# Nine chunks of 64 keys in quarters of the array, five score banks, probabilities turned in place and moved by pairs of units

## Chip, cores, metric

The kernel runs on one core of a Trainium2 chip. The metric is the device time of one execution in microseconds (us). The kernel before has a median of 1205.0 us in three runs (1204.82 to 1205.19).

## What is computed

Thresholded attention over 8 batches and 8 heads with 576 tokens and a head width of 64, followed by a mixer: a token MLP (576 to 256 to 576) and a channel MLP (512 to 1536 to 512), each with a residual. All data are fp32.

```python
scores = scale * np.matmul(q, k.transpose(0, 1, 3, 2))
thresh = np.max(scores, axis=-1, keepdims=True) - tau
scores = np.where(scores >= thresh, scores, -1000000000.0)
...
attn = attn / (np.sum(attn, axis=-1, keepdims=True) + 1e-09)
return np.matmul(attn, v).astype(np.float32)
...
xt = x.transpose(0, 2, 1)
h = np.maximum(xt @ w_tok1, 0.0) @ w_tok2
u = x + h.transpose(0, 2, 1)
h2 = np.maximum(u @ w_ch1, 0.0) @ w_ch2
return (u + h2).astype(np.float32)
```

## The kernel before

**Units, rounds, groups.** Heads are taken two at a time: a pair is two heads, whose 64 channels each lie on partitions 0 to 63 and 64 to 127. Two pairs of a batch have 9 units of 128 queries; the fifth (SHARED) holds the last 64 queries of one pair and the first 64 of the next. Two units are a round (72 in all), three units are a group (six to a batch, 48 in all).

**A round.** `scores_of_two` (L894) multiplies on PE: for each unit, three pieces of 192 keys, both heads, into two tiles of three banks, one for each head; six of the eight PSUM banks are the scores'. A product has 64 rows of the array (one head) and 128 columns; where a round has the shared unit, all its products are cut to 64 columns, that is into quarters of the array. fp32 products run in two passes, and the trace has two records for each. Then DVE takes the maxima, a round and head at a time (L927), POOL makes the bias (L933), ACT subtracts and masks out of PSUM (L943, `mask`) and takes the exponential in place with its sum (L953, `exps`); DVE inverts the sums, POOL scales (L285, `scale`). `e` then has 128 queries on the partitions and 2 x 576 keys.

**Turning e.** In batch 0 PE transposes `e` in blocks of 128 into a bank, and ACT or DVE copies it (L300, L305). In batches 1 to 7 DVE transposes 32x32 blocks from `e` into another tile `T` (L315, `turn_blocks`), and SP issues four transfers of 144 KB for each unit from `T` to `eT` (L327, `move`), after which the partitions hold keys.

**Values.** `values` (L350) makes the weighted sums of a group in one bank: output partitions 0 to 63 for one head, 64 to 127 for the other. A product contracts over 128 keys and fills 64 columns of the array, so that two run side by side. Since 576 keys are four and a half times 128, the fifth chunk of both heads shares one 128-row tile: it is multiplied by a copy of V in which the other head's rows are zero (`split_middle`, L333; its products stand at L365, the others at L370). The middle group of three covers two pairs and does this twice with 192 queries, the others once with 384. ACT or DVE copies the bank out (`values_out`, L372). V is loaded once for each pair, in batches 1 to 7 by four transfers in rows of 256 bytes (L128).

**Order.** Nothing is left to run time: a planner written into the kernel (`Scheduler`) keeps a clock for each engine, starts the earliest operation by the costs and dependencies written beside it, and emits the instructions in that order; the engines then run their queues in order. The mixer of the batch before (token MLP L477 to L515, channel MLP L1067 and L1143) fills PE between rounds and groups, through the two banks that the scores leave. While the planned clock is under 110 us, `keep_warm` (L719) fills planned gaps of PE with transposes (L732). After the last batch's attention the scores' banks go to the rest of the channel MLP (L1528), which the change does not touch.

## Time and profile before

| what | us |
|---|---|
| median of three runs | 1205.0 |
| the profiled execution | 1205.03 |
| its span on the core | 1203.2 |
| PE matmul busy | 1181.3 |
| DVE busy | 898.3 |
| ACT busy | 603.0 |
| POOL busy | 332.6 |

Some lines of the costliest groups (line, engine, operation, output and input by name and shape, count; then busy us, mean ns of one; then idle time before them and what ended it):

```profile
L943 ACT ACTIVATE e<-sc,bias 128x576 f32<-128x576 f32 x288 | 193.9, 743 | 148.9 <-POOL bias L933 147.8
L927 DVE TENSOR_REDUCE mx<-sc 128x2 f32<-128x1152 f32 x144 | 188.1, 1347 | 54.3 <-PE sc L910 54.3
L953 ACT ACTIVATE e<-e,ntau 128x576 f32<-128x576 f32 x288 | 220.4, 779 | 0.1
L315 DVE STREAM_TRANSPOSE T<-e 128x1152 f32<-128x1152 f32 x126 | 170.7, 1363 | 30.7 <-POOL e L285 23.3
```

And from the table of DMA issues (count, size of each, median us from issue to landing):

```profile
eT<-T SPq DMA_DIRECT2D x504, 144.0 KB, 3.0
```

PEld is the loading of weights into PE, which overlaps PE. Matmul records overlap too: two or four products that use different parts of the array run at once, so the mean of one record is not what it costs; the distance between starts is. In an engine's queue an instruction that waits holds up all behind it.

### The profile page before, as it was taken

The numbers are of one execution on the slowest core, as the hardware profiler recorded it, in microseconds if no ns is written. First come the engines' busy times: TensorE is split into PE (matmuls) and PEld (weight loads), VectorE is DVE, ScalarE is ACT, GpSimd is POOL, SyncE is SP. The second block draws the span as 40 slices with busy tenths as digits, with TensorE's granted clock in tenths as the row PEclk, the third lists the DMA queues.
The fourth block names the chain that finished last, engine by engine and source line by source line (L and its number), as shares of the span: only waits on it lengthen the run. The fifth ranks groups of instructions, "written<-read, shape, count | busy, mean of one in ns | idle before, by whom it ended". The sixth has DMA issues, their size and how long they took to land.

```text
span 1203.2 us, 22528 instructions
## 1 busy us (share of the span) xinstructions
PE 1181.3 (98%) x8177; PEld 966.2 (80%) x8177; DVE 898.3 (75%) x1547; ACT 603.0 (50%) x1363; POOL 332.6 (28%) x523
## 2 busy tenths in 40 slices
PE   8888999999999999999999999999999999999998
PEld 7656788777777777776877777787899999999988
DVE  6788996768678768767867855873778587776866
ACT  6988864664566565465555554550232413223230
POOL 3676553334233434433423422330100000000000
PEclk9999999999999999999999999999999999999999
DMA  7656987668778777777876875571310302122020
GB/s 150 131 134 149 246 198 163 153 137 184 171 153 177 184 159 165 191 159 160 204 155 154 185 182 113 148 181 45 92 36 10 86 12 71 36 51 56 16 56 35
DMA packets 327214, 153.03 MB, mean 127 GB/s; under 512 B 224000, under 2 KB 319296, under 8 KB 326976
## 3 DMA queue, kind: packets, MB, share of 16 engines
q1 hardware_dynamic: 324944, 150.86, 54.4%
q8 instruction: 65, 1.06, 0.4%
q10 hardware_dynamic: 2160, 0.74, 0.2%
q14 instruction: 45, 0.37, 0.1%
HBM read 48.50 MB, written 14.68 MB: 53 GB/s over the span
## 4 chain that ended last, share of the span: by engine, by line
PE 90%; DVE 3%; ACT 3%; DMA 2%; issue 1%; POOL 1%; SPq 1%; DVEq 0%; ACTq 0%; POOLq 0%
PE bank L1528 29%; PE bank L1143 14%; PE bank L1067 11%; PE sc L910 11%; PE bank L370 9%; PE bank L508 5%; PE bank L477 4%; PE bank L365 3%; PE bank L1158 2%; DVE mx L927 1%; ACT e L943 1%; DMA w2s<-in_moe_w_tok_dram 1%; ACT e L953 1%; PE bank L490 1%; DMA lk<-in_k_dram 1%
## 5 line engine op out<-in xcount | busy, mean ns | idle before, releaser
L285 POOL TENSOR_SCALAR e<-e,rr 128x576 f32<-128x576 f32 x288 | 217.0, 771 | 188.7 <-DVE rr L277 188.1
L943 ACT ACTIVATE e<-sc,bias 128x576 f32<-128x576 f32 x288 | 193.9, 743 | 148.9 <-POOL bias L933 147.8
L927 DVE TENSOR_REDUCE mx<-sc 128x2 f32<-128x1152 f32 x144 | 188.1, 1347 | 54.3 <-PE sc L910 54.3
L953 ACT ACTIVATE e<-e,ntau 128x576 f32<-128x576 f32 x288 | 220.4, 779 | 0.1
L315 DVE STREAM_TRANSPOSE T<-e 128x1152 f32<-128x1152 f32 x126 | 170.7, 1363 | 30.7 <-POOL e L285 23.3
L1143 PE MATMUL bank<-xT,wc 128*128 128x256 f32 x768 | 176.4, 383 | 0.3
L1143 PEld LDWEIGHTS bank<-xT,wc 128*128 128x128 f32 x768 | 143.3, 190 | 31.0 <-issue 7.0
L910 PE MATMUL sc<-kT,qT 64*128 64x192 f32 (+1 forms) x2112 | 162.4, 329 | 1.6 <-ACT e L943 1.0
L910 PEld LDWEIGHTS sc<-kT,qT 64*128 64x128 f32 (+1 forms) x2112 | 138.4, 167 | 27.7 <-issue 16.7
L370 PE MATMUL bank<-eT,lv 128*64 128x384 f32 (+1 forms) x1024 | 135.0, 406 | 0.0
L370 PEld LDWEIGHTS bank<-eT,lv 128*64 128x64 f32 x1024 | 73.5, 137 | 50.7 <-issue 45.3
L933 POOL TENSOR_SCALAR bias<-mx,toff 128x2 f32<-128x2 f32 x144 | 41.0, 286 | 194.6 <-DVE mx L927 189.6
L1067 PE MATMUL bank<-wc,g 128*128 128x256 f32 x336 | 77.7, 381 | 0.0
L1643 ACT COPY temps<-bank 128x256 f32<-128x256 f32 x90 | 33.5, 372 | 85.5 <-PE bank L1528 85.0
L508 PE MATMUL bank<-w,a 128*128 128x192 f32 (+1 forms) x256 | 72.6, 420 | 1.5 <-ACT eT L305 0.6
L1067 PEld LDWEIGHTS bank<-wc,g 128*128 128x128 f32 x336 | 62.9, 190 | 11.0 <-issue 1.6
L1148 ACT ACTIVATE g<-bank 128x256 f32<-128x256 f32 x58 | 22.2, 383 | 96.1 <-PE bank L1143 95.9
L1528 PE MATMUL bank<-t,wc 128*128 128x256 f32 x240 | 60.0, 379 | 0.0
L1528 PE MATMUL bank<-t,w1s 128*128 128x256 f32 x240 | 60.0, 379 | 0.0
L1528 PE MATMUL bank<-u,wc 128*128 128x256 f32 x240 | 59.8, 379 | 0.0
L508 PEld LDWEIGHTS bank<-w,a 128*128 128x128 f32 x256 | 43.1, 189 | 20.7 <-issue 5.0
L953 ACT ACTIVATION_READ_ACCUMULATOR e<-e,ntau 128x1 f32 x288 | 58.8, 204 | 0.0
(190 smaller groups left out, 1840.3 us busy)
## 6 DMA issues: line engine op xcount, KB each, us to landing
eT<-T SPq DMA_DIRECT2D x504, 144.0 KB, 3.0
w2s<-in_moe_w_ch_dram SPq DMA_DIRECT2D x24, 512.0 KB, 4.0
lk<-in_k_dram SPq DMA_DIRECT2D x122, 72.0 KB, 2.9
ut<-us SPq DMA_DIRECT2D x136, 64.0 KB, 2.1
lq<-in_q_dram SPq DMA_DIRECT2D x120, 72.0 KB, 3.1
lv<-in_v_dram SPq DMA_DIRECT2D x112, 72.0 KB, 2.6
out_dram<-us SPq DMA_DIRECT2D x30, 256.0 KB, 2.3
u<-spill SPq DMA_DIRECT2D x8, 512.0 KB, 4.5
```

The lines of the kernel that those rows point to most:

```text
L285: nc.gpsimd.tensor_scalar(out=eh, in0=eh, scalar1=rr[:, h : h + 1], scalar2=1.0, op0=ALU.mult, op1=ALU.mult)
L315: nc.vector.transpose(out=T.rearrange("p a (c x) -> p c a x", c=NK), in_=e.rearrange("p (c a x) -> p c a x", c=NK, a=4))
L370: nc.tensor.matmul(to[r], lhsT=lv[:, j, :], rhs=e[j], start=False, stop=(c == NI - 1), skip_group_check=True)
L477: nc.tensor.matmul(bank[:, at], lhsT=w1[:, t, P * m : P * m + P], rhs=x(t), start=(n == 0 and t == 0), stop=False, skip_group_check=True,)
L508: nc.tensor.matmul(bank[:, n * i : n * i + n], lhsT=hidden[b][:, m, P * c : P * c + P], rhs=w2[:, m, lo : lo + n], start=(m == 0), stop=(m ...
L910: nc.tensor.matmul(sc[h][rows, f, HT * k : HT * k + HT], lhsT=qT[r, cols], rhs=kT[r, HT * f : HT * f + HT], start=True, stop=True, skip_gr ...
L927: nc.vector.tensor_reduce(out=mx[:, h], in_=sc[h][:, :, 0 : 2 * HT].rearrange("p f (k x) -> p k f x", k=2), axis=AX.XY, op=ALU.max)
L943: nc.scalar.activation(out=eh, in_=part[h], func=AF.Prelu, bias=bias[:, h], scale=SCALE, alpha=STEEP)
L953: nc.scalar.activation(out=eh, in_=eh, func=AF.Exp, bias=ntau, accum_out=rs[:, h, 0:1])
L1067: nc.tensor.matmul(bank[:, 0:HD], lhsT=x[:, j, :], rhs=y[:, j, :], start=j == 0, stop=j == HJ - 1)
L1143: nc.tensor.matmul(bank[:, 0:n], lhsT=wc1[:, j, c, :], rhs=uT[:, c, GR * i : GR * i + n], start=(c == 0), stop=(c == NCC - 1))
L1528: nc.tensor.matmul(to, lhsT=l, rhs=r, start=start and x == 0, stop=x == len(pairs) - 1, skip_group_check=not start)
```

## The change

In batches 1 to 7 the keys are put in another order: K is transposed so that `e` has, for each of 4 x 9 blocks, 16 keys of one head beside 16 of the other. After the turn and the move a chunk has 64 keys of one head on partitions 0 to 63 and the same 64 of the other head on 64 to 127: nine chunks without a rest. `values_of_halves` multiplies each chunk in four products at a time: two heads (rows of the array) by two halves of 192 queries, into two banks. For the second half of a group the heads are crossed, which `side` and `crossed` see to, so that each quarter of the array is used once; V is loaded as it stands and crossed, each by two transfers in rows of 2304 bytes (`load_heads`), and `split_middle` remains for batch 0 alone. Two copies take the halves out.

All scores are made in quarters of the array, by cuts of 128, 384 and 64 keys (64, 384, 128 for the second unit), into one tile of five banks. The third bank holds keys of both heads; a POOL memset (`mark`) stands between the first unit's products there and the second's. The general banks become three. A mask of a round's second unit also waits for the second maximum.

`e` is turned in place and `T` goes; `e` is kept until the move has read it. Units of a batch come in another order, in which two of three rounds hold the first and third unit of a group: these share a tile and are moved together by four transfers. The planner's new operation takes two banks at once.

```diff
-    ps_s2 = attn.enter_context(tc.tile_pool(name="ps_s2", bufs=2, space=bass.MemoryType.PSUM, side="right", reuse_waits="tile"))
+    ps_s2 = attn.enter_context(tc.tile_pool(name="ps_s2", bufs=1, space=bass.MemoryType.PSUM, side="right", reuse_waits="tile"))
...
-    units = [(b, 2 * w, t) for b in range(B) for w in range(NP // 2) for t in range(9)]
+    first_row = [(2 * w, t) for w in range(NP // 2) for t in range(9)]
+    in_turn = (0, 2, 1, 4, 3, 5, 6, 8, 7)
+    paired = [(0, t) for t in in_turn] + [(2, t) for t in (1, 0, 2, 3, 5, 4, 7, 6, 8)]
+    units = [(b, *x) for b in range(B) for x in (paired if b else first_row)]
+    where = {x: u for u, x in enumerate(units)}
...
-                in_=(q, k)[which][b, 2 * p + h, 32 * lo : 32 * hi, 32 * c : 32 * c + 32].rearrange("(n t) d -> t n d", t=32),
+                in_=(q, k)[which][b, 2 * p + h, 32 * lo : 32 * hi, 32 * c : 32 * c + 32].rearrange(
+                    "(t n) d -> t n d" if which and b else "(n t) d -> t n d", t=32
+                ),
...
+    def place_v(name):
+        return att.tile([P, NK, D], F32, tag="lv", bufs=VL + 1, name=name)
...
-        lv = att.tile([P, NK, D], F32, tag="lv", bufs=VL, name=f"lv_{n}")
+        if n not in vals:
+            vals[n] = place_v(f"lv_{n}")
         rows = v[b].rearrange("h s d -> (h s) d")[2 * S * p : 2 * S * p + 2 * S, :]
-        if not b:
-            nc.sync.dma_start(out=lv, in_=rows.rearrange("(c p) d -> p c d", p=P))
-        else:
-            for a in range(4):
-                nc.sync.dma_start(out=lv[a:P:4], in_=rows.rearrange("(c a r) d -> a r c d", a=4, r=32)[a])
-        vals[n] = lv
-
+        nc.sync.dma_start(out=vals[n], in_=rows.rearrange("(c p) d -> p c d", p=P))
+
+    def load_heads(n, crossed):
+
+        b, p = pairs[n]
+        lv = quads[n, crossed] = place_v(f"lv_{n}_{crossed}")
+        for i in range(2):
+            rows = v[b, 2 * p + (1 - i if crossed else i)].rearrange("(a y c) d -> y a (c d)", y=16, a=4)
+            nc.sync.dma_start(out=lv[D * i : D * i + D].rearrange("p c d -> p (c d)"), in_=rows)
+
+    quads = {}
...
+            if which and in_blocks(pairs[n][0]):
+                nc.vector.transpose(
+                    out=heads[n][1].rearrange("p (a c z y) -> p y c a z", a=4, c=NK, z=8),
+                    in_=loaded[n][1].rearrange("p (y c) (a z) -> p y c a z", y=2, a=4),
+                )
+                continue
...
+    def side(u, h):
+        b, p0, t = units[u]
+        return 1 - h if in_blocks(b) and t % GU == 2 else h
+
+    def half(u, e, h):
+        if not in_blocks(units[u][0]):
+            return e[:, S * h : S * h + S]
+        at = 16 * side(u, h)
+        return e[:, :, :, at : at + 16]
...
+    def home_of(u):
+        it, k = divmod(u, 2)
+        if not in_pairs(it):
+            e = att.tile([P, 4, NK, 32], F32, tag="e1", bufs=EM, name=f"e_{u}")
+            return e if in_blocks(units[u][0]) else e.rearrange("p a c x -> p (a c x)")
+        if not k:
+            two[it] = att.tile([P, 4, 2, NK, 32], F32, tag="e2", bufs=EP, name=f"e_{u}")
+        if in_blocks(units[u][0]):
+            return two[it][:, :, k]
+        return two[it].rearrange("p a k c x -> p (a k c x)")[:, 2 * S * k : 2 * S * k + 2 * S]
+
+    EP, EM = 2, 3
...
+    def in_pairs(it):
+        b, p0, t = units[2 * it]
+        return t % GU != 1 if in_blocks(b) else it % 3 != 1
...
-        b, p0, t = units[u]
-        e = st.pop(u)
-        T = Ts[u] = att.tile([P, 4, NK * 32], F32, tag="T", bufs=3, name=f"T_{u}")
-        nc.vector.transpose(
-            out=T.rearrange("p a (c x) -> p c a x", c=NK), in_=e.rearrange("p (c a x) -> p c a x", c=NK, a=4)
-        )
-
-    def move(u):
-        b, p0, t = units[u]
+        e = st[u].rearrange("p a c x -> p a (c x)")
+        nc.vector.transpose(out=e, in_=e)
+
+    def move(us):
+        b, p0, t = units[us[0]]
-        T = Ts.pop(u)
+        if len(us) == 2:
+            e = two[us[0] // 2].rearrange("p a k c x -> p a (k c x)")
+            place = slice(0, GU, 2)
+        else:
+            e = st[us[0]].rearrange("p a c x -> p a (c x)")
+            place = t % GU
         for i in range(4):
-            nc.sync.dma_start(
-                out=turned_e[key][:, place, i, :], in_=T[32 * i : 32 * i + 32]
-            )
+            nc.sync.dma_start(out=turned_e[key][:, place, i, :], in_=e[32 * i : 32 * i + 32])
+        for u in us:
+            st.pop(u)
...
-            if n < NP:
-                nc.gpsimd.tensor_copy(out=vl[r, r], in_=lv[r, NI, :])
-            else:
-                nc.vector.tensor_tensor(
-                    out=vl[:, r].bitcast(I32), in0=lv[:, NI, :].bitcast(I32), in1=whose[:, r], op=ALU.bitwise_and
-                )
+            nc.gpsimd.tensor_copy(out=vl[r, r], in_=lv[r, NI, :])
...
+    HALVES = [((0, 0), (0, HT)), ((0, 2 * HT), (1, 0)), ((1, HT), (1, 2 * HT))]
+
+    def values_of_halves(b, p0, g, banks):
+        lv = [quads[b * NP + p0 + i, half] for half, (i, _) in enumerate(HALVES[g])]
+        M = HT // 32
+        for c in range(NK):
+            for half in range(2):
+                to = banks[half][:, 0:HT].rearrange("p (m x) -> p m x", x=32)
+                for i in range(2):
+                    r, o = [slice(D * x, D * x + D) for x in (i, 1 - i if half else i)]
+                    nc.tensor.matmul(
+                        to[o],
+                        lhsT=lv[half][r, c, :],
+                        rhs=eT[r, M * half : M * half + M, c, :],
+                        start=c == 0,
+                        stop=c == NK - 1,
+                        skip_group_check=True,
+                    )
+
+    def half_out(b, p0, g, half, bank, copy):
+        i, tok = HALVES[g][half]
+        copy(out=xTs[b][:, p0 + i, tok : tok + HT], in_=bank[:, 0:HT])
...
-    sched.banks.extend([Bank(ps_b, "m0"), Bank(ps_b, "m1")])
+    sched.banks.extend([Bank(ps_b, f"m{i}") for i in range(3)])
...
+    def make_heads(Q, m):
+        n = 2 * Q + m // 2
+        if Q < 2 or n >= len(pairs):
+            return
+        free = {0: 3 * Q - (1 if Q == 2 else 2), 1: 3 * Q - (2 if Q == 2 else 1), 2: 3 * Q - 1, 3: 3 * Q}[m]
+        heads_loaded[0] = put(
+            ("heads", Q, m),
+            sched.op("sp", 1.2, lambda: load_heads(n, 1 - m % 2), (key_op("V", free),), 0, after=(heads_loaded[0],), dmas=(2, 147, 0.70)),
+        )
...
+    AT = (0, 5 * MAIN - 2 * S)
+    CUTS = ((0, P, MAIN, S), (0, D, D + 3 * P, S))
+
+    mark = const.tile([P, 1], F32, name="mark")
+
     def scores_of_two(us):
-        sc = [ps_s2.tile([P, 3, MAIN], F32, tag="sc", name=f"sc{h}_{us[0]}") for h in range(2)]
-        split = any(units[u][2] == SHARED for u in us)
+
+        sc = ps_s2.tile([P, 5 * MAIN], F32, tag="sc", name=f"sc_{us[0]}")
+        firsts = []
         for k, u in enumerate(us):
             b, p0, t = units[u]
-                n, step = b * NP + p0 + (t > SHARED), D if split else P
-                parts = [(n, slice(o + i, o + i + step), slice(i, i + step)) for i in range(0, P, step)]
-            for f in range(3):
-                for n, cols, rows in parts:
+                parts = [(b * NP + p0 + (t > SHARED), slice(o + i, o + i + D), slice(i, i + D)) for i in (0, D)]
+            crossed = [in_blocks(b) and t % GU == 1 and i == 1 for i in range(2)]
+            for lo, hi in zip(CUTS[k], CUTS[k][1:]):
+                for c, ((n, cols, rows), cross) in enumerate(zip(parts, crossed)):
                     for h in range(2):
                         r = slice(D * h, D * h + D)
                         qT, kT = heads[n]
-                        nc.tensor.matmul(
-                            sc[h][rows, f, HT * k : HT * k + HT],
+                        slot = 1 - h if cross else h
+                        at = AT[slot] + S * k
+                        x = nc.tensor.matmul(
+                            sc[rows, at + lo : at + hi],
                             lhsT=qT[r, cols],
-                            rhs=kT[r, HT * f : HT * f + HT],
+                            rhs=kT[r, lo:hi],
                             start=True,
                             stop=True,
                             skip_group_check=True,
                         )
+                        if (at + lo) // MAIN == 2:
+                            if k:
+                                behind(x, marked)
+                            else:
+                                firsts.append(x)
+            if not k:
+                marked = nc.gpsimd.memset(mark, 0.0)
+                for x in firsts:
+                    behind(marked, x)
...
-            out=mx[:, h], in_=sc[h][:, :, 0 : 2 * HT].rearrange("p f (k x) -> p k f x", k=2), axis=AX.XY, op=ALU.max
+            out=mx[:, h], in_=sc[:, AT[h] : AT[h] + 2 * S].rearrange("p (k x) -> p k x", k=2), axis=AX.X, op=ALU.max
...
-            e = att.tile([P, 2 * S], F32, tag="e", bufs=4, name=f"e_{u}")
+            e = home_of(u)
-        eh = e[:, S * h : S * h + S].rearrange("p (f x) -> p f x", f=3)
-        nc.scalar.activation(out=eh, in_=part[h], func=AF.Prelu, bias=bias[:, h], scale=SCALE, alpha=STEEP)
+        scores = part[h]
+        if in_blocks(units[u][0]):
+            scores = scores.rearrange("p (a c y) -> p a c y", a=4, c=NK)
+        nc.scalar.activation(out=half(u, e, h), in_=scores, func=AF.Prelu, bias=bias[:, h], scale=SCALE, alpha=STEEP)
...
+        if in_blocks(b):
+            deps += [key_op("heads", G // 3, m) for m in (g, g + 1)]
+            if p0 == 0 and g == 0:
+                deps += xreads.get(b - 2, [])
+            x = put(("V", G), sched.op("pe", VALUES_IN_HALVES, lambda: None, deps, 0))
+            x.fn, x.bank, x.both, x.values = lambda banks: values_of_halves(b, p0, g, banks), True, True, True
+            for half in range(2):
+                y = sched.op(
+                    "act",
+                    0.33,
+                )
+                y.frees, y.half = x, half
+                put(("X", G) if half else ("X", G, 0), y)
+            next_heads(G)
+            return
...
-                    deps += [key_op("T", u - 4), key_op("pre", u - 1, 0)]
+                    deps += used_before(u) + [key_op("pre", u - 1, 0)]
                 else:
                     deps.append(key_op("pre", u, 0))
+                if u % 2:
+                    deps.append(key_op("mx", it, 1))
...
-            put(("T", u), sched.op("dve", 1.31, lambda u=u: turn_blocks(u), deps, 4))
-            put(
-                ("M", u),
-                sched.op(
+            put(("T", u), sched.op("dve", 1.31, lambda u=u: turn_blocks(u), deps + [key_op("T", u - 1)], 4))
+            space = [key_op("V", G - 2) if opens or in_pairs(it) else None]
+            if not in_pairs(it) or u % 2:
+                ws = (u - 1, u) if in_pairs(it) else (u,)
+                x = sched.op(
                     "sp",
                     2.4,
-                    lambda u=u: move(u),
-                    (key_op("T", u), key_op("V", G - 2) if t % GU == 0 else None),
+                    lambda ws=ws: move(ws),
+                    [key_op("T", w) for w in ws] + space,
                     0,
-                    after=(key_op("M", u - 1),),
-                    dmas=(4, 147, 0.69),
-                ),
-            )
-            if t % GU == GU - 1:
+                    after=(key_op("M", ws[0] - 1),),
+                    dmas=(4, 147 * len(ws), 0.69),
+                )
+                for w in ws:
+                    put(("M", w), x)
```

## The prediction

> **What bounds the kernel now.** I read the stages first (busy time of each engine in chosen windows), since a mean over the whole span mixes stages with different limits. The columns are the window, its length, busy time and count for PE, PEld, DVE, ACT and POOL, then the granted clock, the DMA share and GB/s.
>
> ```profile
> 0.00:150.00 150.00, 133.10 (x1049) 99.45 (x1051) 126.74 (x216) 125.84 (x264) 86.11 (x132) 1.00 0.71 162
> 203.00:789.00 586.00, 585.18 (x4089) 450.09 (x4089) 433.01 (x611) 334.76 (x725) 210.22 (x344) 1.00 0.74 165
> 852.00:1203.00 351.00, 347.06 (x2256) 322.50 (x2254) 266.61 (x626) 99.51 (x278) 0.00 (x0) 1.00 0.17 46
> ```
>
> From 203 to 789 us PE idles for 0.8 of 586 us; no other engine is above 74%. Only before 150 us does PE idle (17 us), with DVE and ACT both near 84%. After 852 us no attention runs, and the change leaves that part alone. The chain that ended last says the same:
>
> ```profile
> PE 90%; DVE 3%; ACT 3%; DMA 2%; issue 1%; POOL 1%; SPq 1%; DVEq 0%; ACTq 0%; POOLq 0%
> ```
>
> So between 150 and 850 us a microsecond taken from PE is a microsecond of the span, as long as nothing new makes PE wait. The timeline of PE alone (start, length, line, operation, shape, number of records) prices its pieces:
>
> ```profile
> 301.59 0.55 PE L365 MATMUL bank<-eT,vl 128*64 128x192 f32 x4
> 301.96 1.47 PE L370 MATMUL bank<-eT,lv 128*64 128x192 f32 x16
> 303.26 0.49 PE L365 MATMUL bank<-eT,vl 128*64 128x192 f32 x4
> 303.59 1.47 PE L370 MATMUL bank<-eT,lv 128*64 128x192 f32 x16
> 304.99 2.22 PE L910 MATMUL sc<-kT,qT 64*128 64x192 f32 x24
> 307.14 8.90 PE L1143 MATMUL bank<-xT,wc 128*128 128x256 f32 x40
> 315.97 0.87 PE L365 MATMUL bank<-eT,vl 128*64 128x384 f32 x4
> 316.67 2.75 PE L370 MATMUL bank<-eT,lv 128*64 128x384 f32 x16
> 319.35 1.99 PE L1143 MATMUL bank<-xT,wc 128*128 128x256 f32 x8
> 324.17 2.18 PE L910 MATMUL sc<-kT,qT 64*64 64x192 f32 x48
> 326.29 3.94 PE L1143 MATMUL bank<-xT,wc 128*128 128x256 f32 x17
> ```
>
> From one start to the next: a values group of one pair takes 319.35 - 315.97 = 3.38 us, one of two shares 304.99 - 301.59 = 3.40, a round of scores 307.14 - 304.99 = 2.15, and a round already cut into quarters (64*64, 48 records) 326.29 - 324.17 = 2.12. Every fp32 product leaves two records. In the second line 16 records, two at a time, fill 303.26 - 301.96 = 1.30 us: 0.1625 us for a pair 192 wide. The round in quarters has 48 records, four at a time: 12 x 0.1625 = 1.95 us and 0.17 to start and drain. So four quarters cost what two halves cost: 0.1625 us at 192 columns. At 384 columns a pair takes 0.32 (eight in 2.58 of the chain's "PE bank L370 x16"), so the price is about 0.83 ns a column plus 2.5 ns.
>
> **The values.** Removed per group: five steps of products, the middle one (L365) half zeros. Added: 36 products 192 wide, 72 records, 18 steps of four: 18 x 0.1625 + 0.17 = 3.10 us. Gain 0.28 on the 28 one-pair groups and 0.30 on the 14 with two shares, batches 1 to 7: 12.0 us.
>
> **The scores.** Cuts of 128, 384 and 64 hold the same 576 columns in three steps as three of 192 do: 109 + 322 + 56 = 487 ns against 3 x 162.5. All rounds become quarters; 49 of those after batch 0 were not: 49 x 0.03 = 1.5 us. A 64-wide step was never run; a 64*64 load stands with 133 ns in its row, and if four such steps a round waited for loads in full, 63 rounds would lose 4 x (133 - 56) = 0.31 us each, 19 us. But that round in quarters sustains one step in 162.5 ns with 133 ns loads beside it, and a 128-column load of 190 ns does not hold back products 128 wide that start 112 ns apart in the last stage. I take 0 and keep up to 19 for the range.
>
> **The mark.** Banks fall from six to five; the third bank holds the head of one head's first unit and the tail of the other head's second unit. Four products of the second unit therefore wait for a POOL memset, which waits for the first unit's. The tail starts 1.79 us into the round (1024 columns in two records each, ten steps, and the load); the first cut is done at about 0.3. POOL has 1.4 us for a memset of 0.11 (the row of L253) and two signals that take 0.03 to 0.1 us elsewhere. What can be late is POOL:
>
> ```profile
> 305.03 2.92 POOL L285 TENSOR_SCALAR e<-e,rr 128x576 f32<-128x576 f32 x4 [1.69 <-DVE rr L277]
> L253 POOL MEMSET rs<- 128x4 f32 x4 | 0.2, 107 | 0.1
> ```
>
> Four scalings are 2.92 us, and 13 of the 72 marks stand in the new instruction order right behind two or four scalings of the round before. Had those scalings the times of the same numbers in this trace, they would end up to 8.6 us after the round's start, and what lies past 1.6 us (1.79 less the memset and the signals) would sum to 19 us; if they begin before the round, as their place ahead of the mark suggests, a pair ends by 1.5 us and PE waits for nothing. Nearer the low end: 4 us. Behind a waiting mark stand the scalings and the biases of the next masks; DVE's transposes and ACT wait for these. A wait on PE that is already met costs nothing here: the second L365 group above carries one in mid stream and keeps its 0.1625.
>
> **The start.** In batch 0 the new order has 200 filler transposes (L732 before) in place of 121: the planned order expects more waiting there. Their row gives 0.12 us each, 9.5 us if the rounds come that much later, 0 if they fill the 17 us that PE idled anyway. PE's real work ahead of the tenth round differs by only 2 us between the two orders, and conversion of the weights and ACT, not PE, set the pace there. I take 3. The third general bank could win some of the waits that precede transposes (L300, 8.7 us in its row); I count none.
>
> **Costed at nothing, with the cover.** Turning e in place: the same 1152 elements, 126 x 1.36 us of DVE, which idles 26%. Scaling, masking and exponentials in rows of 16: no row has that shape; copies with rows of 32 (L1088, 373 ns) cost what plain ones do (L1643, 372 ns). Were each ACT pass a quarter slower, 1.5 us a round would come off ACT's idle 43%, and values would be late by it. The 56 bitwise ANDs (11.7 us of DVE) go; up to 53 more small copies (352 ns on DVE) come. K transposed with a step of two elements: at worst 28 x 0.75 us more on DVE, a pair ahead. V loaded twice, 8 MB more at 165 GB/s, is 49 us of DMA over 650, in rows of 2304 bytes in place of 256; it lands a group (16 us) ahead. Moving e by pairs saves 168 issues of 0.6 us on SP, but the burst is twice as long: two units, 1.18 MB, take 7 us at 165 GB/s against 3.6 for the last unit now. In 28 of 42 groups a pair comes last, so values can be 3.5 us late. Cover: MLP work set between (PE waited 0.5 us in all for these transfers). e is also held until its move has landed, about 15 us after its mask; the next user comes two paired rounds, at least 20 us, later.
>
> **Sum.** The profiled execution took 1205.03 us (span 1203.2, 1.8 around it), the median is 1205.0. 1205.0 - 12.0 - 1.5 + 4 + 3 = 1198.5; I predict 1198.
>
> **A rule against it.** In the new values two row tiles write one bank at once: the first head's rows into partitions 0 to 63 and the second's into 64 to 127. In the trace's quarters each row tile has its own bank, so no row tests this. The Trainium skill ("TensorEngine Tiling (Array Packing)", Gotcha 1: PSUM Pressure) says that different row tiles cannot access one PSUM bank at the same time, and gives no price (the last rival is what it would do here); "PSUM — Partial Sum Buffer" (PSUM bank collisions raise a hardware error) adds that different column tiles can, on disjoint partitions.
>
> **Rivals.**
> - Nothing is lost: fillers fill idle time, marks are met. 1205.0 - 13.5 = 1191.5. For: PE idles 0.8 us in 586 now.
> - Values come late behind the longer bursts: 3.5 us in 28 groups is 98 us uncovered; with a tenth of it left, 10 us, 1208.5 on top of this sum, 1201.5 without the other losses. Against: the 0.5 us above.
> - POOL's mark stalls PE (slower): the 19 us bound, with the 3 for the start: 1205.0 - 13.5 + 19 + 3 = 1213.5. It decides once the marks' waits pass 10.5 us (13.5 less the start's 3), 0.8 us in each of the 13 rounds. For: the four-scaling block of 2.92 us; against: the order puts most marks behind work long done.
> - Two row tiles in one bank take turns, so that a step of four takes 0.325: 18 x 0.1625 x 42 = 123 us, and 41 for the 42 crossed score units (0.975 each): 1355. Against: the two tiles write different partitions.
>
> **Chances.** Forecast 0.58 (own range 1194 to 1203), nothing lost 0.16, late values 0.09, the mark 0.13, the shared bank 0.04. The measurement tells no change from one of 0.2%, 2.4 us. Faster by more: nearly all of the first, the second and a third of the third: 0.75; within 0.2%: 0.05; slower: the mark, half of the late values, the bank: 0.20. Range 1189 to 1210: the sum less half of what the start and marks were charged, and up to part of the mark's case; 19 us for narrow steps or a shared bank lie outside.
>
> **What would show it.** A values group at 3.1 us and all score rounds at 2.12 on PE's timeline; PE waiting for POOL's memset in the waits, in few rounds and about 4 us in all; the tenth round not more than 3 us later; L285's successor not far above 771 ns. Values at 6 us, PE idle over 10 us behind the memset or the moves, or the attention ending later than now, would make it wrong.

## The result and the profile after

The changed kernel takes 1257.9 us (median of four runs, 1249.0 to 1261.2), the kernel before beside it 1205.1: a ratio of 1.042, interval 1.040 to 1.044. The forecast was 1198, 7 us faster; it is 53 us slower.

The same windows as before, of the changed kernel (window, length, PE, PEld, DVE, ACT and POOL busy, granted clock, DMA share, GB/s). Its attention ends at 869 us, 53 later, so the last window begins later:

```profile
0.00:150.00 150.00, 136.15 (x1426) 100.95 (x1430) 115.88 (x197) 123.58 (x262) 82.42 (x138) 0.98 0.64 153
203.00:789.00 586.00, 546.33 (x6178) 432.77 (x6178) 396.82 (x536) 305.46 (x671) 195.74 (x367) 0.98 0.76 167
900.00:1255.00 355.00, 351.35 (x2278) 326.48 (x2276) 269.09 (x631) 99.42 (x278) 0.67 (x1) 1.00 0.17 46
```

PE idles for 39.7 us where it idled for 0.8, no other engine is fuller than before, and PE's granted clock is 0.98 where it was 1.00. The chain that ended last stops at 35% PE: further back it could not be followed. Yet the pieces cost what they should. PE's timeline:

```profile
384.71 2.19 PE L1007 MATMUL sc<-kT,qT 64*64 64x128 f32 x48
386.83 1.56 PE L574 MATMUL bank<-w,a 128*128 128x384 f32 x4
...
394.80 2.19 PE L1007 MATMUL sc<-kT,qT 64*64 64x128 f32 x48
396.81 3.10 PE L425 MATMUL bank<-eT,lv 64*64 64x192 f32 x72
399.85 1.57 PE L574 MATMUL bank<-w,a 128*128 128x192 f32 x8
```

A round of scores takes 386.83 - 384.71 = 2.12 us, a values group 399.85 - 396.81 = 3.04. So the time is lost between the pieces. What PE waited for (us in all, times, longest):

```profile
PE bank L425 <- DMA eT<-e: 28.7, 9, 7.9
PE sc L1007 <- ACT e L1050: 8.5, 11, 2.4
PE sc L1007 <- POOL mark L1021: 7.3, 8, 3.1
```

The longest of these, on the timeline of all engines (lines of other work left out; SPq is SP's queue issuing transfers, its length the time that the issues held SP):

```profile
535.70 2.63 DVE L360 STREAM_TRANSPOSE e<-e 128x1152 f32<-128x1152 f32 x2
...
536.55 2.49 SPq L483 DMA_DIRECT2D x_sb<-xs  x4
...
539.09 1.45 SPq L119 DMA_DIRECT2D lq<-in_q_dram  x1
...
540.59 0.61 SPq L119 DMA_DIRECT2D lk<-in_k_dram  x1
...
541.30 3.81 SPq L1242 DMA_DIRECT2D ut<-us  x6
...
543.29 0.78 DVE L283 STREAM_TRANSPOSE kT<-lk 128x576 f32<-128x576 f32 x1 [4.97 <-issue]
...
545.14 0.18 DVE L324 RECIPROCAL rr<-rr 128x4 f32<-128x4 f32 x1
545.21 4.86 SPq L375 DMA_DIRECT2D eT<-e  x4
545.76 2.90 POOL L332 TENSOR_SCALAR e<-e,rr 128x576 f32<-128x576 f32 x4 [1.83 <-DMA ut<-us]
...
553.91 2.52 PE L425 MATMUL bank<-eT,lv 64*64 64x192 f32 x28 [7.92 <-DMA eT<-e]
```

Two units are turned by 538.33. Their move stands in SP's queue behind the issues shown and begins at 545.21, 6.9 us later. Its four issues hold SP for 4.86 us (the forecast reckoned 0.6 each), and PE idles 7.92 us until they have landed. Meanwhile K's block, issued at 540.59, holds up DVE until 543.29 (the row names no releaser, but DVE's wait for that transfer ends at 543.25 in the trace). What stands behind it there, the inverse of the sums, ends only at 545.32, and POOL's scalings of the next round begin at 545.76. Their row names a landing of `ut` as what ended the wait; it came at 545.36, so either of the two can have been the last. The kernel before does such a stretch like this, eight issues for two units in 5.10 us:

```profile
492.01 5.10 SPq L327 DMA_DIRECT2D eT<-T  x8
```

After such a gap PE also gets fewer clocks (the last three numbers of a window are granted clock, DMA share and GB/s):

```profile
540.00:545.00 5.00, 4.78 (x52) 3.63 (x54) 1.71 (x4) 3.35 (x11) 0.10 (x1) 1.00 0.42 82
545.00:550.00 5.00, 0.98 (x20) 0.58 (x12) 3.02 (x6) 0.00 (x0) 2.93 (x5) 1.00 0.75 134
550.00:555.00 5.00, 1.09 (x16) 0.99 (x20) 2.42 (x2) 2.23 (x4) 0.51 (x2) 0.59 0.88 224
555.00:560.00 5.00, 5.00 (x72) 4.01 (x64) 0.69 (x2) 1.06 (x3) 0.00 (x0) 0.73 0.65 111
```

**The account.** "Attention" is here from the first values of batch 1 to the last of batch 7; "idle" adds PE's gaps over 0.15 us, "clock" PE's busy time times what was missing of the clock, in windows of 5 us.

| | first values of batch 1 at | attention | idle in it | clock | after it |
|---|---|---|---|---|---|
| before | 137.6 | 678.9 | 0.5 | 0 | 386.7 |
| changed | 147.2 | 721.8 | 50.4 | 13.2 | 386.3 |

The span grew by 52.2: 9.6 at the start, 42.9 in the attention, -0.4 behind it. The 42.9 are 49.9 of idle and 13.2 of clock, less 20.2 of other time. The gain on PE is there, 13.5 foreseen; the 7 more I can't separate from work moved ahead of the first values.

**Where it falls.** The starts of values groups, set against the starts that the kernel's own planner reckoned, tell where the order comes apart. Before, values start 3.3 us behind the planner's clock in batch 1 and 1.0 at the end. Changed, it is 11.5 and 61.2, and 46 of these 50 us arise between the fifth group of a batch and the first of the next (4.1, 4.4, 9.5, 8.3, 6.9, 9.0, and 4.0 before the last group of all). There SP has most to issue: moves, the next heads' Q, K and V, and the mixer's transfers.

**SP's queue.** The page does not count issuing as busy. Summed over SP's records from 150 us to 852 us (before) and to 900 us (changed):

| | issues | us of issues | moves | K | mixer's ut | from the last turn to the move's first issue |
|---|---|---|---|---|---|---|
| before | 917 | 565 | 0.63 each | 0.59 | 0.59 | 2.45 (mean) |
| changed | 766 | 620 | pairs 1.20, units 0.66 | 0.78 | 0.78 | 4.47 |

Of four paired issues the first two hold SP for 0.70 and 0.75 us in the mean, the third and fourth for 1.64 and 1.73; from the first issue to the last landing such a move takes 8.78 us (33 moves whose landing the trace tells), a unit's 5.25 before. So 151 fewer issues cost SP 55 us more. The moves themselves take SP as long as before (300 us, then 303); the rest of the 55 us is in the other issues, 439 before and 442 after, that stand among them. Between issues SP pauses mostly under 0.1 us. With its pauses under 0.15 us counted, SP is occupied from 150 us to the end of the attention for 562 + 49 of 667 us before and 619 + 43 of 719 in the changed kernel: 92% in both, and in the changed kernel 90 to 100% between a batch's fifth values group and the next batch's first. The attention has grown as SP's work has.

### The profile page after: what moved, and what is told of

Read it like the earlier page. It is cut to its first block, busy times and chain, and to the rows that moved or that the text cites. A ratio compares the mean times of both kernels' runs of the same rounds, so it can differ in the third digit from the quotient of the medians.

```text
span 1255.4 us, 29091 instructions
## 1 busy us (share of the span) xinstructions
PE 1186.8 (95%) x11504; PEld 986.8 (79%) x11504; DVE 888.7 (71%) x1501; ACT 603.0 (48%) x1380; POOL 339.6 (27%) x591
## 5 line engine op out<-in xcount | busy, mean ns | idle before, releaser
L360 DVE STREAM_TRANSPOSE e<-e 128x1152 f32<-128x1152 f32 x126 | 170.2, 1361 | 24.4 <-POOL e L332 21.5
L1007 PE MATMUL sc<-kT,qT 64*64 64x128 f32 (+2 forms) x3456 | 163.1, 330 | 18.4 <-ACT e L1050 8.5
L425 PE MATMUL bank<-eT,lv 64*64 64x192 f32 x3024 | 146.0, 341 | 32.7 <-DMA eT<-e 28.7
L1007 PEld LDWEIGHTS sc<-kT,qT 64*64 64x64 f32 x3456 | 97.8, 134 | 85.6 <-issue 45.0
L425 PEld LDWEIGHTS bank<-eT,lv 64*64 64x64 f32 x3024 | 125.6, 141 | 49.8 <-issue 17.5
L1021 POOL MEMSET mark<- 128x1 f32 x72 | 7.4, 102 | 194.9 <-PE sc L1007 185.5
L1174 PE MATMUL bank<-w2s,g 128*128 128x256 f32 x252 | 58.6, 382 | 0.1
```

What stands on the lines that cost most here:

```text
L360: nc.vector.transpose(out=e, in_=e)
L425: nc.tensor.matmul(to[o], lhsT=lv[half][r, c, :], rhs=eT[r, M * half : M * half + M, c, :], start=c == 0, stop=c == NK - 1, skip_group_che ...
L1007: x = nc.tensor.matmul(sc[rows, at + lo : at + hi], lhsT=qT[r, cols], rhs=kT[r, lo:hi], start=True, stop=True, skip_group_check=True,)
L1174: nc.tensor.matmul(bank[:, 0:HD], lhsT=x[:, j, :], rhs=y[:, j, :], start=j == 0, stop=j == HJ - 1)
```

## Experiments

Three theories. Q: SP's queue. M: the mark, by which POOL and PE wait for each other. H: `e` is held until its move has landed. L and B, named in some expectations, are that the order has no slack anywhere, and that the bytes as such are late. Every ratio is against the kernel before on the same chip. But for the first, all runs up to the two reliefs together (e18) keep the changed kernel's order of instructions, so that only the chip's times differ.

**The planner's price.** `dmas=(4, 147 * len(ws), 0.69)` becomes 1.25 for a pair.

> Theory Q (SP's queue): an issue of a pair's move (288 KB) holds SP for 1.21 us in the mean where the kernel's planner reckons 0.69, SP has no idle time at the end of a batch, and everything behind on it (K's loads, the next move) comes 4 to 5 us late there; DVE's transposes of K and then the values wait. Here only the planner's price is changed, to 1.25 us, so that PE's order has other work where the values would be late. Q expects the last values group of the attention to be no more than 10 us further behind the planner's clock than the first group of batch 1 (50 us in the changed kernel), PE to wait under 12 us for moves, and 1215 to 1235 us. Theory M (POOL's mark between the two units of a round stalls PE and the scalings behind it) and theory H (e is held until its move has landed and two buffers of pairs are too few) expect the drift to stay over 30 us and 1245 us or more.

1266.6 us, 1.050 (1.048 to 1.053): a miss for Q, and within what M and H expected. PE waits 17.1 us for moves in place of 28.7, but the drift is still 43 us. In the new order SP issues from 612 to 670 us with hardly a pause over 0.1 us: the planner paces PE by SP, and whatever holds an issue longer than planned is never made up. A right price alone does not mend it.

**Moves by units, same order.**

```diff
...
-        for i in range(4):
-            nc.sync.dma_start(out=turned_e[key][:, place, i, :], in_=e[32 * i : 32 * i + 32])
+        for u in us:
+            e = st[u].rearrange("p a c x -> p a (c x)")
+            for i in range(4):
+                nc.sync.dma_start(out=turned_e[key][:, units[u][2] % GU, i, :], in_=e[32 * i : 32 * i + 32])
```

> The same instruction order as the changed kernel, but each pair's four issues of 288 KB become eight of 144 KB. If SP's time for a move goes with its bytes once several are under way, eight cost as much as four (8 x 0.62 = 5.0 us against 4.9), and theory Q expects 1250 to 1265 us, with the same groups late. If it is the size of one transfer that holds SP, the eight go faster than the four and the time falls by 10 us or more. M and H expect no change beyond 3 us.

1236.7 us, 1.026 (1.023 to 1.029): 21 us back from the move alone, with the same bytes and 168 issues more. Eight issues hold SP as long as the four (0.65 us each), but the first four need only the first unit's turn, and what follows goes faster (K 0.67, the mixer 0.64). M and H expected no change. PE's wait for moves falls to 11.6 us:

```profile
PE bank L421 <- DMA eT<-e: 11.6, 5, 3.3
```

**The mark, six in a row.**

```diff
                 for x in firsts:
                     behind(marked, x)
+                for _ in range(5):
+                    marked = nc.gpsimd.memset(mark, 0.0)
```

> The mark becomes six POOL memsets in a row, about 0.5 us longer in each of 72 rounds, all else and the order as in the changed kernel. Q: PE waits for the mark in few rounds, so at most 10 us more (1255 to 1267). M: the wait for the mark decides in most rounds, so 0.5 us x 63 = 30 us more, 1285 or above.

1264.2 us, 1.048 (1.044 to 1.051), 6 more. PE waits for it twice as long:

```profile
PE sc L1007 <- POOL mark L1025: 14.5, 11, 2.9
```

M falls as the main cause.

**One issue for V.** Two issues of 64 partitions become one of 128: `rows = v[b, 2 * p : 2 * p + 2].rearrange("h (x c) d -> (h x) (c d)", c=NK)`.

> Both heads of V are loaded by one issue in place of two, in the plain order of rows (the values are then formed from wrongly ordered rows of V, so the output is not the reference's; bytes and instructions of all other engines are the same). The order is that of the changed kernel. SP has 56 issues of some 0.75 us less, 42 us over seven batches. Q: batch ends are 2 to 3 us less late, 1232 to 1247 us. M and H: within 4 us of 1257.

1238.7 us, 1.027 (1.025 to 1.029): 19 us from 56 issues of SP, no other engine's instruction touched. Q is borne out.

**V's, and Q's and K's loads from ACT's queue.** `nc.sync` becomes `nc.scalar` in `load_heads`, or in `load_qk` from batch 1's second pair on.

> The order of the changed kernel, paired moves kept; the 112 issues of V's loads are made by ACT's queue (its own DMA queue) in place of SP's. SP has 75 us of issues less between 150 and 900 us (106 x 0.71), ACT about as much more, of which it idles 43%. Output as the reference. Q: like the one issue for both heads (1238.7 us), 1230 to 1245. Theory B (what is late is the bytes on the DMA engines, whoever issues them): the same bytes are moved, so 1252 to 1262.

> Both reliefs at once, in the same order: moves by units (1236.7 us alone) and V's loads from ACT's queue. Q: the gains add in part, 1215 to 1228. B: no better than 1234.

> The order of the changed kernel, paired moves kept; the loads of Q and K of batch 1's second pair and all later ones go to ACT's queue: 134 us of SP's issues (75 for K, 59 for Q) less. K's blocks then land without standing behind the moves, so DVE should not wait for them (27.9 + 9.0 us in the changed kernel) and the scalings, turns and moves behind DVE come in time. Q: below 1230 us, and DVE's wait for K under 10 us. If the loads were not what delays DVE and the moves alone are late, 1240 to 1250. The danger is ACT's own queue: a load that waits for DVE there holds up masks and exponentials; then 1255 or more.

> Moves by units, V's and Q's and K's loads all on ACT's queue, the same order: SP is left with about 400 of its 600 us of issues after 150 us. Q: the drift against the planner's clock after batch 0 (50 us in the changed kernel) falls below 12 us, so 1200 to 1218 us, if ACT bears 190 us more; M and H: above 1230.

1271.4, 1251.0, 1320.2 and 1371.7 us: all worse than without (1257.9 for the paired, 1236.7 for the units' moves), where Q had expected gains in all four. SP is relieved as meant (549 us of issues in the first), but ACT's queue is in order too, and its copies, masks and exponentials now stand behind transfers that wait. ACT in the first, and DVE waiting for ACT's exponentials in the third (55.0 us in the changed kernel):

```profile
ACT xT L436 <- DMA lv<-in_v_dram: 15.2, 3, 10.7
```

```profile
DVE rr L323 <- ACT e L1060: 125.7, 48, 8.8
```

I had named the danger for Q and K only. These runs do not tell Q from B; they show that ACT has no room where these loads fall, though it idled 43% of the stretch from 203 to 789 us before the change.

**Both reliefs of SP together (e18):** moves by units and one issue for V.

> Moves by units (20.5 us gained alone) and one issue for both heads of V, rows in plain order so that the output is not the reference's (18.6 us gained alone); the order of the changed kernel. Theory Q, that the time is lost behind SP's queue at the ends of the batches: the two add up to most of their sum, 1216 to 1224 us. Theory L (no engine by itself; the order leaves no slack between the rounds, so every wait of 1 to 3 us anywhere is kept): 1228 to 1236.

1215.7 us, 1.007 (1.005 to 1.009). 1257.9 - 21 - 19 = 1218: the two add up, which L did not expect. The windows from 203 to 789 us, of units alone, of one V issue alone, and of both:

```profile
203.00:789.00 586.00, 563.27 (x6447) 443.98 (x6446) 411.01 (x556) 314.88 (x692) 202.94 (x379) 0.98 0.74 172
```

```profile
203.00:789.00 586.00, 556.58 (x6369) 441.71 (x6371) 407.69 (x551) 314.76 (x692) 200.83 (x374) 0.98 0.78 172
```

```profile
203.00:789.00 586.00, 572.40 (x6630) 454.45 (x6629) 425.04 (x573) 324.06 (x712) 209.45 (x391) 0.99 0.76 177
```

PE idles for 22.7, 29.4 and 13.6 us. In the last one its wait for the mark is down as well, without the mark being touched, so most of the 7.3 us was lateness from elsewhere:

```profile
PE sc L1002 <- POOL mark L1016: 1.6, 2, 1.2
```

**Planned anew: in place by units, out of place, in a ring of seven.** Each keeps the values in quarters, five banks, the mark and the order of units; moves are by units at 0.63 us. From the ring's edit:

```diff
...
-            two[it] = att.tile([P, 4, 2, NK, 32], F32, tag="e2", bufs=EP, name=f"e_{u}")
...
+        e = att.tile([P, 4, NK, 32], F32, tag="e", bufs=7, name=f"e_{u}")
...
```

> e is still turned in place and held until it has landed, but each unit is moved by itself and the order is planned anew with that, at 0.63 us an issue (what units' issues measured). Q: 1205 to 1225, since the order now knows SP's time. Theory H (the hold) and L: like the units in the old order, 1230 to 1245.

> As the run before, but e is turned into a tile of its own (four buffers for e, three for the turned ones, as in the kernel before), so that e's buffer is free at the turn and not after the landing; K's loads are planned 2 us more cautiously. Values in quarters, scores in five banks, the mark and the new order of units stay. H: ACT no longer waits for moves (22 us in the changed kernel, 18 to 42 in the others), 1200 to 1215. If the hold costs nothing: within 8 us of the run before.

> e in place in a ring of seven tiles of one unit, each freed by its own landing; moves by units at 0.63 us an issue; values planned 1.5 us more cautiously after a landing. The same hold as in the changed kernel with the same memory, but no pair waits for its second half. H in its weak form (pairs hold each other): 1205 to 1220. L: 1225 or more.

1235.5, 1241.4 and 1236.0 us (1.023, 1.027, 1.024; each within 0.004). Q missed the first (1205 to 1225): an order that knows SP's price gains nothing over the old order with units (1236.7), as L had expected of it and of the ring. It doesn't take work from SP, which by the sums above is still occupied for 93, 93 and 91% of the time to the attention's end. Freeing `e` at the turn, the second, gains nothing over holding it, so H is not borne out, although ACT waits 17.8 us for moves in the first (22.4 in the changed kernel). The orders differ between these runs, so it is not excluded that the hold costs a few us.

**Q and K in fewer, larger issues (e22 to e25).** Both 32-column halves of a head in one issue of 144 KB; in the second kernel also V by one issue where it isn't crossed; the last two planned anew on top of that.

```diff
+                eng[which].dma_start(
+                    out=loaded[n][which][D * h : D * h + D].rearrange("p n d -> p (n d)"),
+                    in_=(q, k)[which][b, 2 * p + h].rearrange("x (c d) -> c x d", c=2),
...
```

> Moves by units (1236.7 us), the order of the changed kernel, and Q and K of batches 1 to 7 loaded by two issues of 144 KB each in place of four of 72 KB (Q's rows go to the partitions as K's do, and DVE's transpose puts them back in order). SP has 112 issues of 0.6 to 0.67 us less, some 70 us, if an issue of twice the packets still takes about 0.65; the bytes and packets are the same. Q: 1212 to 1224 us. If an issue's time goes with its packets of 128 bytes, 1.3 us each, nothing is saved: 1232 to 1242. L: 1228 or more in both cases.

> As e22, and the uncrossed one of V's two loads is one issue for both heads (28 issues less), with K's columns ordered so that V's rows are read in plain order and the result is the reference's. SP has about 90 us of issues less than with moves by units alone. Q: 1203 to 1216 us, and PE idle under 15 us between the first values of batch 1 and the last of batch 7 (31 us with units alone, 20 with one V issue). L: no more than 3 us below e22.

> The joined loads of e23 with the order planned anew, each issue at its measured price; e turned into a tile of its own, freed at the turn; values planned 3.5 us and K's transposes 2 us more cautiously than in the changed kernel. Values in quarters, five banks for the scores, mark and order of units stay. Q: SP no longer binds, PE is the bound again and the 20 us of PE work saved in the attention show: 1188 to 1204 us. L or H: above 1212.

> The same joined loads and measured prices, e in place in seven tiles of a unit, held until landed; values planned 1.5 us more cautiously. Q: 1190 to 1206 us. H: at least 10 us above e24.

1653.7, 1638.9, 1668.8 and 1672.7 us. None of the expectations held. SP's timeline in the first:

```profile
1011.41 0.56 SPq L118 DMA_DIRECT2D lk<-in_k_dram  x1
1012.03 5.39 SPq L118 DMA_DIRECT2D lq<-in_q_dram  x1
1017.47 5.45 SPq L118 DMA_DIRECT2D lk<-in_k_dram  x1
1023.03 5.41 SPq L384 DMA_DIRECT2D eT<-e  x1
```

One joined issue is let through; whatever comes behind waits 5.4 us, and DVE waits 202 us for K. A window with such a load under way, and one a little later with moves of units alone:

```profile
1018.00:1023.00 5.00, 4.76 (x77) 3.59 (x75) 4.32 (x5) 0.82 (x2) 2.14 (x4) 1.00 0.17 27
1031.00:1033.00 2.00, 0.14 (x2) 0.17 (x4) 2.00 (x3) 0.00 (x0) 0.00 (x0) 0.50 0.86 240
```

The joined load moves 27 GB/s, and 144 KB at 27 GB/s are 5.4 us: what comes behind waits as long as the load takes. V's halves are as large, with 16 outer steps in the source, and held SP for 0.64 us each in the run with moves by units; the joined source has 2 outer steps. No run shows which DMA engines worked. The Trainium skill ("DMA: Bandwidth & Descriptors", section "Why a DMA increments its semaphore by 16 and not by 1") says that a transfer uses as many engines, up to 16, as divide the slowest dimensions of both sides, which would be two here: the DMA share of 0.17 in place of 0.86 agrees with few engines, but doesn't tell how many.

**SP relieved further, same order.** As the two reliefs together, and every second pair of heads keeps the Q and K before it (`if n > NP and n % 2: return` in `load_qk`): 112 issues less.

> As e18 (moves by units, one issue for V in plain order), and every second pair of heads from batch 1 on keeps the Q and K of the pair before it: 112 issues of 72 KB less, some 70 us of SP (what is left out are those loads, so the output is not the reference's; all instructions of the other engines and their order stay). Q: PE waits under 12 us between the first values of batch 1 and the last of batch 7, its clock is granted in full there, and the time is 1194 to 1206, the prediction's sum with a start that costs 9 in place of 3 us. L: 1210 to 1216, no better than e18.

1208.3 us (1203.0 to 1211.1 in ten runs), 1.002 (1.000 to 1.003): 7 us better again, 2 us slower than Q expected and 2 us faster than L. Its trace is of the fastest of the ten executions, 1203.0 us. From 203 to 789 us:

```profile
203.00:789.00 586.00, 575.85 (x6732) 456.11 (x6728) 430.64 (x582) 332.60 (x731) 213.48 (x397) 1.00 0.69 167
```

The attention takes 673.0 us, 5.9 less than before the change, with 16 us of idle and 2.8 of clock still in it, and its first values come at 141.9. From turn to move it is 2.47 us, as in the kernel before, and SP is occupied for 80% of the time to the attention's end.

**The kernel before with 56 issues more.** Two of the four issues of each of V's loads are cut in two; the same bytes, the same order.

> The kernel before, its order unchanged; two of the four issues of each of V's loads are cut in two (56 issues more, the same bytes, 34 us more of SP's time over seven batches). SP issues for 565 of the 702 us from 150 to 852 us there, with about 0.08 us between one issue and the next 91% of its time. If SP was near its limit already (Q), the attention ends 3 us later or more: 1208 to 1222 us. If it had room for 34 us and only the changed kernel's order binds it: 1204 to 1207.

1227.6 us, 1.019 (1.016 to 1.022): 22 us slower, more than Q expected.

```profile
203.00:789.00 586.00, 570.82 (x3985) 438.62 (x3985) 415.04 (x585) 323.57 (x704) 203.46 (x333) 1.00 0.71 159
```

PE, which idled 0.8 us there, idles 15.2. SP is occupied for 95% of the time to the attention's end, which comes 23 us later. SP was near its limit before the change already: it had no room for 56 issues.

No run beats the kernel before; the best that loads everything, and in its right order, takes 1235.5 us.

## Why the prediction was wrong

**The step that failed** stands under "Costed at nothing": "Moving e by pairs saves 168 issues of 0.6 us on SP". It took 101 us off SP at the price of a unit's issue and so took SP for free. Four issues of a pair hold SP about as long as the eight they replace would (1.20 us each against 0.63), nothing was saved, and with what they hold up SP issues for 55 us more. Behind it stands the first reading, "no other engine is above 74%": the issuing queue is not in that table. SP was occupied for 92% of the time to the attention's end, and the run with 56 more issues shows that little of the rest was slack. There were two bounds, PE and SP, and the page shows one of them. Of the prediction's own signs, PE idle behind the moves (28.7 us) and an attention that ends later both came.

- *Values and scores.* Foreseen 3.10 and 2.12 us, measured 3.04 and 2.12. Narrow cuts cost nothing, as taken.
- *Moves by pairs.* "Values can be 3.5 us late" was right in size: 8.78 - 5.25 = 3.5 us from issue to landing. That a pair comes last in 28 of 42 groups was a misreading: in the order of units it is so in three of the six groups of a batch, 21, and the rival's full price 74 us in place of 98. The cover was not: the late-values rival had 10 us, the moves alone cost 21. Its evidence, PE's 0.5 us of waiting before, held for moves that left SP 2.45 us after the turn.
- *V loaded twice.* "It lands a group ahead" is beside the point: it was priced in bytes, and what V asks of SP is issues. These are as many as before (104, then 106 in the windows of SP's table), twice as large, and take 75 us in place of 67. That halving them gains 19 us tells what SP's time is worth, not what the second load costs.
- *The mark.* 4 us charged, 7.3 measured, of which 1.6 remain when SP is relieved by units and one issue for V. The rival that stalled PE by it is not what happened.
- *The start.* 3 charged (0 to 9.5). The tenth round's maxima come at 99.9 in place of 93.3 us, the first values of batch 1 9.6 us later; with SP relieved most it is 4.3.
- *In place, and rows of 16.* Turns 1361 ns, masks 741, exponentials 782, scalings 774 (before 1363, 743, 779 and 771): nothing, as taken.
- *The hold.* ACT waited 22.4 us for landings, where none was foreseen; no run makes it a cause.
- *The shared bank.* Two row tiles in one bank on different partitions ran four at a time, 18 steps in 3.04 us. The Trainium skill's sentence ("TensorEngine Tiling (Array Packing)", Gotcha 1: PSUM Pressure) does not hold there; the measurement decides.
- *The clock* was not in the sum at all: 13 us, a consequence of the gaps.

**What stays open.** From 1208 to 1198 some 10 us are left; the trace of the fastest execution (1203.0) has 16 us of PE idle in several waits of up to 3 us (masks, weight conversion, copies, moves). Moves by units and one issue for V leave the bytes as they are, which speaks against B, and so do the 56 issues added to the kernel before; the last relief drops bytes as well. SP's time and the landing of K can't be told apart in the same-order runs. Why SP's other issues take longer among paired moves no run shows.

## What to carry to other kernels

Sum the issuing time of each DMA queue, pauses included, before calling an engine the only bound; the busy table leaves it out. Price a joined transfer by what it holds the queue for when several follow each other, and look at the outermost step of its source. When a part sits idle for half its time, ask still whether it has room where the work bunches: SP had none at the ends of batches, and ACT none where the loads were put on it.

## What the runs showed of the hardware

- In the changed kernel's attention the granted clock was down to 0.50 to 0.71 in a window of 5 us after each of eight PE gaps of 2.8 us or more; after gaps of 1.5 and 2.4 us it stayed at 1.00. In other runs the length of one gap did not decide: with SP relieved further the clock fell to 0.66 after gaps of 0.84 and 2.02 us with 0.54 us of work between them, and in the kernel before with 56 issues more it stayed at 1.00 after one of 3.12 us. The Trainium skill ("TensorE: Matmul & The Clock Gate", section "HAM oscillation — how this bites in real kernels") puts the limit at about 3.4 us; here shorter gaps went either way. The two cases from other runs, and their windows:

```profile
807.50 0.54 PE L422 MATMUL bank<-eT,lv 64*64 64x192 f32 x4 [0.84 <-DMA eT<-e]
810.06 2.36 PE L422 MATMUL bank<-eT,lv 64*64 64x192 f32 x36 [2.02 <-DMA eT<-e]
810.00:815.00 5.00, 4.94 (x69) 4.67 (x70) 0.08 (x1) 0.32 (x1) 0.00 (x0) 0.66 0.70 216
```

```profile
432.31 1.99 PE L1145 MATMUL bank<-xT,wc 128*128 128x256 f32 x8 [3.12 <-DVE rr L278]
430.00:435.00 5.00, 2.69 (x20) 2.26 (x24) 2.79 (x6) 0.60 (x2) 2.28 (x4) 1.00 0.92 212
435.00:440.00 5.00, 5.00 (x63) 4.27 (x56) 4.55 (x5) 1.56 (x4) 1.16 (x3) 1.00 0.51 106
```

- The third and fourth of four issues of 288 KB in a row hold SP for 1.64 and 1.73 us. 288 KB in 1.7 us is 173 GB/s, close to what the DMA engines moved on the whole (167); that SP then waits for them to drain fits, but no run shows what it waits for.
- DVE's transpose of Q took 1228 ns (mean, with Q's loads joined) with results 72 bytes apart, and 742 ns in the changed kernel.
